# Attention then a gated feed-forward: four heads to a group, paired score matmuls, column-tiled values, and the two halves woven together

## Chip, cores, metric

One core of one Trainium2 chip. The metric is the device time of one execution in microseconds (us), the median of several runs.

## What is computed

Eight batches, 12 heads, 448 positions, head width 64, all inputs float32. The attention output, heads side by side (768 wide), feeds a gated feed-forward of inner width 1024. The result is float32, 8 x 448 x 768.

```python
q_n, k_n = rmsnorm(q, g_q), rmsnorm(k, g_k)        # over the head width
scores = (1 / sqrt(64)) * q_n @ k_n.T
attn = softmax(scores)
x = (attn @ v)                                      # heads side by side: 448 x 768
h = maximum(x @ w_in, 0)                            # 448 x 1024
u, v = h[..., :512], h[..., 512:]
v_n = (v - mean(v)) / sqrt(var(v) + 1e-6)
v_s = w_spatial @ v_n + b_spatial[:, None]          # mixes the 448 positions
out = (u * v_s) @ w_out
```

## The kernel before, in words

The kernel is written in a tile framework: the code gives the instructions, their tiles and an order of priority, and a scheduler fixes each engine's instruction queue ahead of the run. Each engine then works through its queue in order and waits on semaphores. Tiles come from pools with a fixed number of buffers. PE is TensorE, DVE VectorE, ACT ScalarE, POOL GpSimd, SP the queue that issues most DMAs.

It has two halves that follow each other. Constants and weights come first (L52 to L97): the weights are loaded as bfloat16 through POOL's DMA queue, and the spatial weights are transposed on TensorE.

*Attention* (L117 to L248) loops over batches and, inside, over heads. `prep_pair` (L118) loads q, k and v of two heads as bfloat16 with six POOL DMAs (L123, L126, L132), squares q and k on POOL (L143, L144), sums the squares on VectorE (L145, L148), takes Ln and Exp on ScalarE for the reciprocal root (L151, L153), scales q and k on VectorE (L162, L167), and transposes them on TensorE, two heads to 128 rows (L174, L179); VectorE copies them out of PSUM (L184, L185). A head's scores (L226) are four matmuls of 64 rows by 448 columns in two halves; the two matmuls of a half belong to the same head, so they use the same 64 rows of the array. ScalarE takes the exponential of each half (L232). No maximum is subtracted, since both operands are normalised. `emit_pv` (L191) multiplies by the values one head later: four matmuls whose stationary operand is 112 x 65, the 65th column being ones, so that row 64 of the result is the sum of the softmax (L195). The result leaves PSUM on ScalarE (L203) or VectorE (L206), and two SP DMAs carry it and the row of sums to DRAM (L207, L209).

*Between the halves* (L250 to L256) all sums are read back, inverted at once on VectorE, and written to DRAM.

*The gated half* (L266 to L360) loops over batches: x and the reciprocals, the latter broadcast to 64 rows each, are loaded from DRAM (L268 to L277) and multiplied (L279). `ps_uu` (L288) is u transposed, `ps_vv` (L306) is v; ScalarE applies Relu to both (L294, L312). VectorE takes the statistics (L315, L316), ScalarE Ln and Exp of the variance (L317, L319), VectorE normalises (L322). `ps_s` (L333) mixes the positions; the bias enters through a 113th row. VectorE multiplies by u (L339), `ps_oo` (L349) is the output projection, ScalarE copies it out (L355) and SP stores it (L357).

ScalarE's function tables are loaded by the compiler where a function is not in the active set; Ln and Exp alternate.

## Time and profile before

| | |
|---|---|
| three runs | 677.19, 679.34, 679.83 us (median 679.34) |
| span of the profiled execution | 677.2 us |
| PE busy | 548.9 us, 1936 matmuls |
| ACT busy | 388.2 us |
| POOL busy | 323.8 us |
| DVE busy | 277.4 us |
| DMA | 47.50 MB in 160417 packets |
| mean granted clock of PE | 0.979 |

The profiled execution's own time is its span from the first to the last instruction; no time outside it is listed. A line of the group list reads: source line, engine, operation, output <- inputs, shape of output <- input, count, then total busy us and mean ns of one, then the engine's idle time just before these instructions and what ended it. A line of a timeline reads: start in us, length in us, engine, line, operation, shape, count; several like instructions in a row are merged, and their length is from the first start to the last end. A matmul's end is modelled, so the distance between the starts of consecutive matmuls says more about the rate of the array than the length of one.

### The profile page before, as it was taken

How to read it: one execution, taken by the hardware profiler on the slowest of the kernel's cores; microseconds unless marked ns; L12 is line 12 of the kernel's file. 1: busy time of each engine (PE TensorE's matmuls, PEld its weight loads, DVE VectorE, ACT ScalarE, POOL GpSimd, SP SyncE). 2: the span in 40 equal slices, each digit the busy share in tenths (PEclk: the TensorE clock that was granted, in tenths of full speed). 3: DMA queues.
4: the chain of work that ended last, by engine and by line, in shares of the span. 5: the costliest groups of instructions: out<-in, count | busy, mean ns of one | idle time of the engine just before them, and what ended most of it. 6: DMA issues, size and time to landing. Idle time of an engine off the chain costs nothing.

```text
span 677.2 us, 6343 instructions
## 1 busy us (share of the span) xinstructions
PE 548.9 (81%) x1936; PEld 224.7 (33%) x1936; DVE 277.4 (41%) x519; ACT 388.2 (57%) x532; POOL 323.8 (48%) x452
## 2 busy tenths in 40 slices
PE   0167989798989989989979979992688898898875
PEld 0122332333333223233233223230344554464433
DVE  0167353643445355265255255232334234333331
ACT  0057676866876777676676686571244534544441
POOL 5799959595858867778678642002010011011000
PEclk9999999999999999999999999999988988999889
DMA  8978868675857776787577541002933532523022
GB/s 129 100 51 62 65 49 66 51 60 40 65 42 55 59 61 54 56 62 56 48 55 59 46 37 21 15 14 59 206 103 102 163 103 68 157 84 100 26 76 81
DMA packets 160417, 47.50 MB, mean 70 GB/s; under 512 B 136335, under 2 KB 156032, under 8 KB 160384
## 3 DMA queue, kind: packets, MB, share of 16 engines
q0 software_dynamic: 135520, 19.32, 41.2%
q1 hardware_dynamic: 24864, 27.79, 14.9%
q8 instruction: 15, 0.25, 0.1%
q14 instruction: 18, 0.15, 0.1%
HBM read 49.68 MB, written 16.69 MB: 98 GB/s over the span
## 4 chain that ended last, share of the span: by engine, by line
PE 61%; ACT 23%; DMA 6%; issue 4%; POOL 3%; DVE 2%; SPq 0%; DVEq 0%; ACTq 0%; POOLq 0%
PE ps_scores L226 20%; PE ps_o L195 18%; PE ps_s L333 6%; PE ps_oo L349 5%; PE ps_vv L306 5%; ACT L151 5%; ACT expT L232 5%; ACT L153 4%; PE ps_uu L288 4%; DMA w_sp_bf<-in_moe_w_spatial_dram 2%; DMA out_dram<-out_sb 2%; PE ps_t L179 2%; ACT lms_sb L151 2%; ACT out_sb L355 2%; PE ps_t L174 2%
## 5 line engine op out<-in xcount | busy, mean ns | idle before, releaser
L232 ACT ACTIVATE expT<-ps_scores 112x896 bf16<-112x896 f32 x192 | 174.0, 915 | 119.1 <-PE ps_scores L226 118.8
L226 PE MATMUL ps_scores<-qkT 64*112 64x448 bf16 x384 | 185.3, 592 | 27.1 <-ACT expT L232 14.5
L195 PE MATMUL ps_o<-expT,v_bf 112*65 112x448 bf16 x384 | 178.9, 579 | 2.9 <-ACT expT L232 2.8
L299 POOL MEMSET vn_sb<- 17x2048 bf16 x8 | 14.3, 1800 | 193.2 <-DVE xT_sb L279 112.3
L226 PEld LDWEIGHTS <-qkT 64*112 64x112 bf16 x384 | 53.3, 189 | 128.1 <-issue 101.0
L195 PEld LDWEIGHTS <-v_bf 112*65 112x65 bf16 x384 | 44.8, 155 | 103.8 <-issue 91.7
L355 ACT ACTIVATE out_sb<-ps_oo 112x768 f32<-112x768 f32 x32 | 26.0, 811 | 86.8 <-PE ps_oo L349 76.8
L132 POOL DMA_DIRECT2D v_bf<-in_v_dram x96 | 67.3, 706 | 12.7 <-DMA w_in_sb<-in_moe_w_in_dram 5.9
L206 DVE CAST xTu<-ps_o 65x448 bf16<-65x448 f32 x48 | 29.7, 619 | 103.4 <-PE ps_o L195 103.4
L123 POOL DMA_DIRECT2D q_raw<-in_q_dram x96 | 68.2, 710 | 5.0 <-DVE q_bf L162 2.6
L126 POOL DMA_DIRECT2D k_raw<-in_k_dram x96 | 69.2, 721 | 0.3
L333 PE MATMUL ps_s<-w_spT_sb,vn_sb 112*128 112x448 bf16 (+1 forms) x128 | 40.7, 463 | 23.7 <-DVE vn_sb L322 23.7
L288 PE MATMUL ps_uu<-xT_sb,w_in_sb 128*128 128x448 bf16 x192 | 44.6, 367 | 18.0 <-DVE xT_sb L279 18.0
L144 POOL TENSOR_TENSOR k_sq<-k_raw 112x512 bf16<-112x512 bf16 x48 | 50.9, 1060 | 16.4 <-DVE ms_sb L148 16.3
L143 POOL TENSOR_TENSOR q_sq<-q_raw 112x512 bf16<-112x512 bf16 x48 | 51.2, 1067 | 14.5 <-DVE ms_sb L145 14.1
L162 DVE SCALAR_TENSOR_TENSOR q_bf<-q_raw,rstd_sb 112x512 bf16<-112x512 bf16 x48 | 42.3, 882 | 26.7 <-ACT rstd_sb L153 25.0
L349 PE MATMUL ps_oo<-w_out_sb,gatedT_sb 128*112 128x384 bf16 x256 | 49.0, 326 | 4.9 <-ACT out_sb L355 4.7
L184 DVE COPY qkT<-ps_t 128x448 bf16<-128x448 bf16 x48 | 18.7, 389 | 83.4 <-PE ps_t L179 82.6
L315 DVE BATCH_NORM_STATS2 stats<-v_sb 112x6 f32<-112x512 bf16 x32 | 22.2, 693 | 66.6 <-ACT v_sb L312 66.6
L306 PE MATMUL ps_vv<-w_in_sb,xT_sb 128*112 128x512 bf16 x192 | 45.2, 379 | 0.4 <-ACT v_sb L312 0.4
L151 ACT ACT_TABLE_LOAD x34 | 43.6, 1283 | 1.3 <-PEq L375 0.7
L174 PE MATMUL ps_t<-identity,q_bf 112*128 112x112 bf16 x192 | 28.3, 295 | 17.8 <-DVE q_bf L162 17.7
(45 smaller groups left out, 511.8 us busy)
## 6 DMA issues: line engine op xcount, KB each, us to landing
out_dram<-out_sb SPq DMA_DIRECT2D x32, 336.0 KB, 2.7
v_bf<-in_v_dram POOLq DMA_DIRECT2D x96, 56.0 KB, 2.9
q_raw<-in_q_dram POOLq DMA_DIRECT2D x96, 56.0 KB, 2.7
k_raw<-in_k_dram POOLq DMA_DIRECT2D x96, 56.0 KB, 2.7
xT_dram<-xTu SPq DMA_DIRECT2D x96, 56.0 KB, 1.9
xT_sb<-xT_dram SPq DMA_DIRECT2D x8, 672.0 KB, 4.5
rec_bc<-rec_dram SPq DMA_DIRECT2D x16, 336.0 KB, 4.8
w_in_sb<-in_moe_w_in_dram POOLq DMA_DIRECT2D x1, 1536.0 KB, 11.5
```

What stands on the lines that cost most here:

```text
L123: pool_eng.dma_start(out=q_raw[:, :, hi, :], in_=q[b, hA + hi].rearrange("(c p) d -> p c d", p=P))
L126: pool_eng.dma_start(out=k_raw[:, :, hi, :], in_=k[b, hA + hi].rearrange("(c p) d -> p c d", p=P))
L132: pool_eng.dma_start(out=v_bf[:, hi, :, 0:D], in_=v[b, hA + hi].rearrange("(c p) d -> p c d", p=P))
L143: pool_eng.tensor_tensor(out=q_sq, in0=q_raw3, in1=q_raw3, op=ALU.mult)
L151: act.activation(out=lms_sb, in_=ms_sb, func=AF.Ln, bias=eps_col[0:P, :], scale=1.0 / D)
L195: pe.matmul(out=ps_o[:, 0:S], lhsT=v_bf[:, hi, jc, :], rhs=expT[:, jc, :], start=(jc == 0), stop=(jc == NCH - 1),)
L226: pe.matmul(out=ps_scores[:, jj, 0:S], lhsT=qkT_cur[p0:p0 + D, 1, jc * P:(jc + 1) * P], rhs=qkT_cur[p0:p0 + D, 0, :], start=True, stop=True,)
L232: act.activation(out=expT[:, 2 * half:2 * half + 2, :], in_=ps_scores[:, :, 0:S], func=AF.Exp, bias=0.0, scale=1.0,)
L288: pe.matmul(out=ps_uu, lhsT=w_in_sb[:, hc, ft * 128:(ft + 1) * 128], rhs=xT_sb[:, hc, :], start=(hc == 0), stop=(hc == NHD - 1),)
L306: pe.matmul(out=ps_vv, lhsT=xT_sb[:, hc, tcc * P:(tcc + 1) * P], rhs=w_in_sb[:, hc, DHALF:DF], start=(hc == 0), stop=(hc == NHD - 1),)
L333: pe.matmul(out=ps_s, lhsT=vn_sb[0:kp, sc, dt * 128:(dt + 1) * 128], rhs=w_spT_sb[0:kp, sc, :], start=(sc == 0), stop=(sc == NCH - 1),)
L349: pe.matmul(out=ps_oo[:, half, 0:DM // 2], lhsT=gatedT_sb[:, dc, tcc * P:(tcc + 1) * P], rhs=w_out_sb[:, dc, half * (DM // 2):(half + 1) * ...
```

## The change

It is a rewrite of the whole kernel function.

- Heads are handled in groups of four, three groups to a batch (24 in all); group g of a batch takes heads g, g+3, g+6 and g+9. q and k are loaded as float32 by SP, one DMA each for a group, three groups ahead; v by POOL, one DMA for a batch. Positions are split so that a partition holds four neighbouring ones, 1 KB in one piece.
- POOL squares q and k and also scales them (both on 1024 float elements of a partition at a time); VectorE sums the squares.
- The two score matmuls issued together now belong to the two heads of a pair, on rows 0 to 63 and 64 to 127 of the array, each into its own bank of PSUM; one exponential serves both.
- The sums come from separate matmuls with a stationary block of ones, 112 x 32, and the values from two half-width calls; each such call is 16 matmuls, four heads on four strips of 32 columns. The reciprocal is Exp(-Ln(sum)) on ScalarE, and VectorE multiplies by it as it takes the values out of PSUM. x stays on chip; the trip through DRAM and the stage between the halves are gone.
- ScalarE's table set is preloaded by name, one that has both Ln and Exp. Relu moves to VectorE.
- The gated part of a batch is cut into 21 units (v, normalisation, u, spatial, output), which are put into the instruction order between the steps of the next batch's attention: each of a group's eight steps adds 0.8 to an allowance, and units are taken while it is above zero, each subtracting its own figure. The first units are taken at the fifth step of the group after the batch's last. The last batch's units run alone at the end.
- PSUM is divided once: two score tiles of two banks, four one-bank tiles for all other uses.

Cut to its core:

```diff
--- before.py
+++ after.py
...
+    act.preload_act_table_set("natural_log_exp_and_others")
...
+    ps_sc = ctx.enter_context(tc.tile_pool(name="ps_sc", bufs=2, space=PSUM))
+    ps_w = ctx.enter_context(tc.tile_pool(name="ps_w", bufs=4, space=PSUM))
...
+    def load_qk(G):
+        b, g = divmod(G, NG)
+        qf = qk_pool.tile([P, 4, NC * D], FP, name="qf")
+        kf = qk_pool.tile([P, 4, NC * D], FP, name="kf")
+        sync.dma_start(out=qf, in_=q_g[b][g])
+        sync.dma_start(out=kf, in_=k_g[b][g])
+        raw[G] = (qf, kf)
...
-                for half in range(2):
-                    ps_scores = ps_sc.tile([P, 2, 512], FP, name="ps_scores")
-                    for jj in range(2):
-                        jc = 2 * half + jj
-                        pe.matmul(
-                            out=ps_scores[:, jj, 0:S],
-                            lhsT=qkT_cur[p0:p0 + D, 1, jc * P:(jc + 1) * P],
-                            rhs=qkT_cur[p0:p0 + D, 0, :],
-                            start=True, stop=True,
-                        )
-                    act.activation(
-                        out=expT[:, 2 * half:2 * half + 2, :],
-                        in_=ps_scores[:, :, 0:S],
-                        func=AF.Exp, bias=0.0, scale=1.0,
-                    )
...
+    def squares(G, i):
+        if i == 0:
+            sqs[G] = st_pool.tile([P, 2, 16], FP, name="ms")
+        t = sq_pool.tile([P, 4, NC * D], FP, name="sqt")
+        pool.tensor_tensor(out=t, in0=raw[G][i], in1=raw[G][i], op=ALU.mult)
+        dve.tensor_reduce(out=sqs[G][:, i, :],
+                          in_=t.rearrange("p l (c d) -> p (l c) d", d=D),
+                          axis=AX.X, op=ALU.add)
+    def rstd(G):
+        ln = st_pool.tile([P, 2, 16], FP, name="lnms")
+        rs = st_pool.tile([P, 2, 16], FP, name="rs")
+        act.activation(out=ln, in_=sqs[G], func=AF.Ln, bias=eps[0:P, :], scale=1.0 / D)
+        act.activation(out=rs, in_=ln, func=AF.Exp, bias=0.0, scale=-0.5)
+        rst[G] = rs
+    def scaled(G, i):
+        t = qn_pool.tile([P, NC, 4, D], BF, name=f"n{i}")
+        pool.tensor_tensor(
+            out=t.rearrange("p c l d -> p l c d"),
+            in0=raw[G][i].rearrange("p l (c d) -> p l c d", d=D),
+            in1=rst[G][:, i, :].rearrange("p (l c) -> p l c", c=NC).to_broadcast([P, 4, NC, D]),
+            op=ALU.mult)
+        nrm[G, i] = t
+    def transposes(G, pr):
+        ps = ps_w.tile([128, 8, 128], BF, name="ps")
+        for i in range(2):
+            for c in range(NC):
+                pe.matmul(out=ps[:, 4 * i + c, 0:P],
+                          lhsT=nrm[G, i][:, c, 2 * pr:2 * pr + 2, :],
+                          rhs=ident[0:P, 0:P], is_transpose=True,
+                          start=(i == 0 and c == 0), stop=(i == 1 and c == NC - 1))
+        t = qt_pool.tile([128, 2, NC, P], BF, name=f"qkt{pr}")
+        dve.tensor_copy(out=t[:, 0], in_=ps[:, 0:4, 0:P])
+        dve.tensor_scalar(out=t[:, 1], in0=ps[:, 4:8, 0:P], scalar1=g2_col, scalar2=None,
+                          op0=ALU.mult)
+        qkt[G, pr] = t
...
+    def scores(G, n):
+        pr, c = divmod(n, NC)
+        ps = ps_sc.tile([P, 2, 512], FP, name="pss")
+        t = qkt[G, pr]
+        for h in range(2):
+            pe.matmul(out=ps[:, h, 0:S],
+                      lhsT=t[64 * h:64 * h + 64, 1, c, :],
+                      rhs=t[64 * h:64 * h + 64, 0, :, :].rearrange("p c s -> p (c s)"),
+                      start=True, stop=True)
+        sct[G, n] = ps
+    def expo(G, n):
+        pr, c = divmod(n, NC)
+        if c == 0:
+            exps[G, pr] = e_pool.tile([P, NC, 2, S], BF, name="et")
+        act.activation(out=exps[G, pr][:, c, :, :], in_=sct[G, n][:, :, 0:S],
+                       func=AF.Exp, bias=0.0, scale=1.0)
...
+    def sums(G):
+        ps = ps_w.tile([128, 512], FP, name="ps")
+        for c in range(NC):
+            for l in range(4):
+                pe.matmul(out=ps[32 * l:32 * l + 32, 0:S], lhsT=ones,
+                          rhs=exps[G, l // 2][:, c, l % 2, :],
+                          start=(c == 0), stop=(c == NC - 1), tile_position=(0, 32 * l))
+        lr = r_pool.tile([128, S], FP, name="lr")
+        rc = r_pool.tile([128, S], FP, name="rc")
+        act.activation(out=lr, in_=ps[:, 0:S], func=AF.Ln, bias=0.0, scale=1.0)
+        act.activation(out=rc, in_=lr, func=AF.Exp, bias=0.0, scale=-1.0)
+        rec[G] = rc
+    def values(G, half):
+        b, g = divmod(G, NG)
+        if g == 0 and half == 0:
+            xts[b] = x_pool.tile([128, 6, S], BF, name="xt")
+        ps = ps_w.tile([128, 512], FP, name="ps")
+        for c in range(NC):
+            for l in range(4):
+                pe.matmul(out=ps[32 * l:32 * l + 32, 0:S],
+                          lhsT=vb[b][:, 3 * l + g, c, 32 * half:32 * half + 32],
+                          rhs=exps[G, l // 2][:, c, l % 2, :],
+                          start=(c == 0), stop=(c == NC - 1), tile_position=(0, 32 * l))
+        dve.tensor_tensor(out=xts[b][:, 2 * g + half, :], in0=ps[:, 0:S], in1=rec[G], op=ALU.mult)
...
+    def unit_v(b, c):
+        if c == 0:
+            vs[b] = m_pool.tile([P, NC, DH], BF, name="vs")
+            sts[b] = m_pool.tile([P, NC, 2], FP, name="mv")
+        ps = ps_w.tile([128, 512], FP, name="ps")
+        for j in range(6):
+            pe.matmul(out=ps[0:P, :], lhsT=xts[b][:, j, c * P:(c + 1) * P],
+                      rhs=w_in[:, j, DH:DF], start=(j == 0), stop=(j == 5))
+        dve.tensor_relu(out=vs[b][:, c, :], in_=ps[0:P, :])
+        s6 = st_pool.tile([P, 6], FP, name="s6")
+        dve.bn_stats(out=s6, in_=vs[b][:, c, :])
+        dve.bn_aggr(out=sts[b][:, c, :], in_=s6)
+    def unit_ln(b):
+        lv = st_pool.tile([P, NC], FP, name="lv")
+        rv = st_pool.tile([P, NC], FP, name="rv")
+        act.activation(out=lv, in_=sts[b][:, :, 1], func=AF.Ln, bias=eps[0:P, :], scale=1.0)
+        act.activation(out=rv, in_=lv, func=AF.Exp, bias=0.0, scale=-0.5)
+        for c in range(NC):
+            dve.tensor_scalar(out=vn_t[b % 2][0:P, c, :], in0=vs[b][:, c, :],
+                              scalar1=sts[b][:, c, 0:1], scalar2=rv[:, c:c + 1],
+                              op0=ALU.subtract, op1=ALU.mult)
...
+    def unit_o(b, c, half):
+        if half == 0:
+            osb[b, c] = o_pool.tile([P, DM], FP, name="osb")
+        ps = ps_w.tile([128, 512], FP, name="ps")
+        for f in range(4):
+            pe.matmul(out=ps[0:P, 0:384], lhsT=gts[b][:, f, c * P:(c + 1) * P],
+                      rhs=w_out[:, f, 384 * half:384 * half + 384],
+                      start=(f == 0), stop=(f == 3))
+        act.activation(out=osb[b, c][:, 384 * half:384 * half + 384], in_=ps[0:P, 0:384],
+                       func=AF.Copy, bias=0.0, scale=1.0)
+        if half == 1:
+            sync.dma_start(out=out[b].rearrange("(p c) m -> c p m", c=NC)[c], in_=osb[b, c])
...
+    NGT = B * NG
+    work = deque()
+    def moe_units(b):
+        for c in range(NC):
+            work.append((1.35, lambda c=c: unit_v(b, c)))
+        work.append((0.0, lambda: unit_ln(b)))
+        for f in range(4):
+            work.append((1.2, lambda f=f: unit_u(b, f)))
+        for f in range(4):
+            work.append((0.8, lambda f=f: unit_s(b, f)))
+        for c in range(NC):
+            for h in range(2):
+                work.append((0.66, lambda c=c, h=h: unit_o(b, c, h)))
+    def prep(G):
+        squares(G, 0)
+        squares(G, 1)
+        rstd(G)
+        scaled(G, 0)
+        scaled(G, 1)
+    prep(0)
+    load_weights()
+    prep(1)
+    transposes(0, 0)
+    scores(0, 0)
+    scores(0, 1)
+    transposes(0, 1)
+    debt = 0.0
+    for G in range(NGT + 1):
+        for n in range(8):
+            if G < NGT:
+                expo(G, n)
+                m, Gn = (n + 2) % 8, G + (n + 2) // 8
+                if Gn < NGT:
+                    scores(Gn, m)
+            if n == 0 and G + 3 < NGT:
+                load_qk(G + 3)
+            if n == 0 and G % NG == 0 and G // NG + 1 < B:
+                load_v(G // NG + 1)
+            if G > 0:
+                if n == 0:
+                    sums(G - 1)
+                elif n == 1:
+                    values(G - 1, 0)
+                elif n == 2:
+                    values(G - 1, 1)
+            if G + 1 < NGT:
+                if n == 3:
+                    transposes(G + 1, 0)
+                elif n == 5:
+                    transposes(G + 1, 1)
+            if G + 2 < NGT:
+                if n == 0:
+                    squares(G + 2, 0)
+                elif n == 1:
+                    squares(G + 2, 1)
+                elif n == 3:
+                    rstd(G + 2)
+                elif n == 4:
+                    scaled(G + 2, 0)
+                elif n == 6:
+                    scaled(G + 2, 1)
+            if G == 1 and n >= 4:
+                w_sp_unit(n - 4)
+            if G > 0 and G % NG == 0 and n == 4:
+                moe_units(G // NG - 1)
+            debt += 0.8
+            while work and debt > 0:
+                cost, fn = work.popleft()
+                debt -= cost
+                fn()
+            debt = min(debt, 0.8)
+    while work:
+        work.popleft()[1]()
```

The units that are left out, `unit_ln`, `unit_u` and `unit_s`, have the matmuls of the old gated half, in the same shapes; `unit_u` has Relu on VectorE.

More of the change, by code (lines that the diff above doesn't have):

```diff
@@ L2 @@
 import math
+from collections import deque
 from contextlib import ExitStack
@@ L6 @@
 import concourse.tile as tile
-from concourse import bass_utils, mybir
+from concourse import mybir
 from concourse.masks import make_identity
@@ L14 @@
 ALU = mybir.AluOpType
+AX = mybir.AxisListType
+PSUM = bass.MemoryType.PSUM
 @with_exitstack
```

365 lines of the change are left out of this document (90 added, 275 removed).

## The prediction

> **What bounds the kernel now.** I read the page first, then the group list with shapes apart, then one line's instructions, then short timelines of TensorE, and the stage windows last. The page:
>
> ```profile
> span 677.2 us, 6343 instructions
> PE 548.9 (81%) x1936; PEld 224.7 (33%) x1936; DVE 277.4 (41%) x519; ACT 388.2 (57%) x532; POOL 323.8 (48%) x452
> ...
> PE 61%; ACT 23%; DMA 6%; issue 4%; POOL 3%; DVE 2%; SPq 0%; DVEq 0%; ACTq 0%; POOLq 0%
> ```
>
> TensorE is the busiest engine and holds 61% of the chain that ended last, ScalarE 23%. A busy TensorE may still be a slow one, so the next views ask at what rate it runs: the score line's instructions, a stretch of the chain in order of time, and TensorE's timeline in attention.
>
> ```profile
> L226 PE MATMUL ps_scores<-qkT x384: 527/577/620, 39.3 to 458.4; 64*112 64x448 bf16 x192
> ```
> ```profile
> 429.98 1.49 PE ps_o L195 x4
> ```
> ```profile
> 431.40 0.99 PE L226 MATMUL ps_scores<-qkT 64*112 64x448 bf16 x2
> 432.32 0.95 PE L195 MATMUL ps_o<-expT,v_bf 112*65 112x448 bf16 x2
> 433.21 0.99 PE L226 MATMUL ps_scores<-qkT 64*112 64x448 bf16 x2
> ```
>
> Attention lasts from 39.3 to 458.4, so 4.37 us a head for 96 heads. Four matmuls of 448 columns take 1.49 us, 0.373 each. Two of scores and two of values come round in 433.21 - 431.40 = 1.81 us; less 4 x 0.373 that leaves 0.32 us, 0.16 for each change between the 64-row and the 112-row shape. The same engine in the gated half:
>
> ```profile
> 602.46 1.46 PE L349 MATMUL ps_oo<-w_out_sb,gatedT_sb 128*112 128x384 bf16 x8
> 603.75 4.05 PE L306 MATMUL ps_vv<-w_in_sb,xT_sb 128*112 128x512 bf16 x18
> 607.64 2.81 PE L288 MATMUL ps_uu<-xT_sb,w_in_sb 128*128 128x448 bf16 x14
> 613.22 1.06 PE L333 MATMUL ps_s<-w_spT_sb,vn_sb 112*128 112x448 bf16 x4 [2.77 <-DVE vn_sb L322]
> ```
>
> Here 18 matmuls of 512 columns take 607.64 - 603.75 = 3.89 us, 0.216 each; in proportion 448 columns cost 0.189, half of attention's 0.373; eight of 384 take 1.29, 0.161 each. So attention runs at half the array rate. No score matmul there is shorter than 527 ns, so it never changes. The window view:
>
> ```profile
> 430.00:460.00 30.00, 28.61 (x77) 8.74 (x76) 7.23 (x14) 20.90 (x27) 0.00 (x0) 1.00 0.06 14
> ```
>
> The clock column says 1.00 for that stretch, which the spacing contradicts; I go by spacing. PE is busy 28.61 of 30 us and still slow. By the Trainium skill ("TensorE: Matmul & The Clock Gate", Part 1) some 3.4 us of sustained activity release the full clock; the trace disagrees for 420 us. By that rule the woven part would be fast, as forecast below, and the groups without gated work would drop from 12 us to nearer ScalarE's 8.2, some 13 us in all. My own reading is that the filled part of the array counts: a score matmul holds 64 of 128 rows, a value matmul 65 of 128 columns, the gated ones nearly all.
>
> **The change, per batch of three groups (12 heads).** All terms are at the full rate first.
>
> TensorE. Scores: 48 matmuls, issued as pairs on rows 0-63 and 64-127; if a pair runs together, 24 x 0.189 = 4.5 us (9.1 if not; no row shows two at once). Shape changes: scores interrupt other work 24 times, two changes each, and nine column-tiled calls add about six: 54 x 0.16 = 8.6 us, taken as the slow clock showed it, with 0 as the lower end. The Trainium skill ("TensorEngine Tiling (Array Packing)", Key Properties) says that a change of tiling mode drains the engine: a rule against this change, and the 0.16 agrees. Sums and values: three calls a group of 16 matmuls on four 32-column strips, 144 in all; if four run together, 36 x 0.189 = 6.8 us, else 27.2. The Trainium skill ("TensorE: Matmul & The Clock Gate", Part 3) gives 2.38x for three strips; by that share of the ideal the 6.8 would be an estimated 8.6, and no run here shows it. I take 6.8. Transposes: 48, priced from
>
> ```profile
> 206.12 0.56 PE L174 MATMUL ps_t<-identity,q_bf 112*128 112x112 bf16 x4
> 206.47 0.58 PE L179 MATMUL ps_t<-identity,k_bf 112*128 112x112 bf16 x4
> ```
>
> as 0.35/4 = 0.088 slow, 0.044 if halved; I take 0.075, 3.6 us. Gated part: 24 x 0.216 + 24 x 0.189 + 16 x 0.189 + 32 x 0.161 = 17.9 us. Sum 41.4 us, 13.8 a group; without shape changes 32.8, 10.9 a group. The rows for the other engines:
>
> ```profile
> L232 ACT ACTIVATE expT<-ps_scores 112x896 bf16<-112x896 f32 x192 | 174.0, 915 | 119.1 <-PE ps_scores L226 118.8
> L151 ACT ACT_TABLE_LOAD x34 | 43.6, 1283 | 1.3 <-PEq L375 0.7
> L153 ACT ACT_TABLE_LOAD x24 | 30.8, 1283 | 0.4
> L355 ACT ACTIVATE out_sb<-ps_oo 112x768 f32<-112x768 f32 x32 | 26.0, 811 | 86.8 <-PE ps_oo L349 76.8 <-DMA out_dram<-out_sb 6.1 <-PE ps_vv L306 3.9
> L203 ACT ACTIVATE xTu<-ps_o 65x448 bf16<-65x448 f32 x48 | 25.9, 539 | 1.0 <-PE ps_o L195 1.0
> ...
> L151 ACT ACTIVATE lms_sb<-ms_sb,eps_col 112x16 f32<-112x16 f32 x48 | 13.2, 303 | 33.7 <-DVE ms_sb L148 33.3
> L232 ACT ACT_TABLE_LOAD x10 | 12.8, 1283 | 0.6 <-PE ps_scores L226 0.4
> L317 ACT ACT_TABLE_LOAD x8 | 10.3, 1283 | 0.1
> L319 ACT ACT_TABLE_LOAD x8 | 10.3, 1283 | 0.1
> L153 ACT ACTIVATE rstd_sb<-lms_sb 112x16 f32<-112x16 f32 x48 | 8.7, 209 | 0.3
> ```
> ```profile
> 205.48 1.73 ACT L232 ACTIVATE expT<-ps_scores 112x896 bf16<-112x896 f32 x2
> ```
>
> ScalarE. Back to back the 915 ns exponential costs 1.73 - 0.915 = 0.82. Per batch 24 x 0.82 = 19.6; three reciprocals as Ln and Exp at 0.54 each, 3.2; four small Ln-Exp pairs at 0.303 + 0.209, 2.0; eight half-width output copies, between 0.41 (half of 811) and 0.54, say 0.48, 3.8. Sum 28.6 us, 9.5 a group. The 84 table loads (108 us) go, if the one preloaded set serves Ln and Exp; Relu moves to VectorE.
>
> ```profile
> L145 DVE TENSOR_REDUCE ms_sb<-q_sq 112x8 f32<-112x512 bf16 x48 | 32.5, 678 | 22.3 <-POOL q_sq L143 11.6 <-ACT lms_sb L151 10.7
> ...
> L315 DVE BATCH_NORM_STATS2 stats<-v_sb 112x6 f32<-112x512 bf16 x32 | 22.2, 693 | 66.6 <-ACT v_sb L312 66.6
> L185 DVE TENSOR_SCALAR qkT<-ps_t,g2g_col 128x448 bf16<-128x448 bf16 x48 | 21.2, 442 | 0.0
> L339 DVE SCALAR_TENSOR_TENSOR gatedT_sb<-ps_s,uT_sb 128x448 bf16<-128x448 f32 x32 | 20.0, 624 | 14.8 <-PE ps_s L333 14.3
> L184 DVE COPY qkT<-ps_t 128x448 bf16<-128x448 bf16 x48 | 18.7, 389 | 83.4 <-PE ps_t L179 82.6
> ...
> L322 DVE TENSOR_SCALAR vn_sb<-v_sb,mv_sb,rstd_ln 112x512 bf16<-112x512 bf16 x32 | 11.1, 410 | 25.9 <-ACT rstd_ln L319 25.9
> L316 DVE BATCH_NORM_AGGREGATE mv_sb<-stats 112x2 f32<-112x6 f32 x32 | 5.8, 182 | 1.1
> ```
> ```profile
> L143 POOL TENSOR_TENSOR q_sq<-q_raw 112x512 bf16<-112x512 bf16 x48 | 51.2, 1067 | 14.5 <-DVE ms_sb L145 14.1
> ```
>
> VectorE. Six sums of squares over 1024 elements at up to 2 x 0.678, 8.1; six pairs of 0.389 + 0.442, 5.0; 18 reads of PSUM at 0.624 (the two value halves of each group, four Relu of u, four products, four Relu of v), 11.2; four of 0.693 + 0.182 + 0.410, 5.1. Sum 29.4 us, 9.8 a group. POOL: squares and scaling are 12 products of 1024 float elements at 2 x 1.067 = 2.13, so 25.6 us, 8.5 a group; if float elements cost double the bf16 ones, 51 us, 17 a group. By the Trainium skill ("GPSIMD Engine Reference", Performance versus the Vector engine), 4497 ns for 2048 float elements, the estimate would be 2.25 us each and 27 us a batch; no run here shows float. I take 25.6. The loads of q and k leave POOL's queue for SP's, where only the output stores stand with them; they are issued three groups ahead, so SP waiting for a free buffer holds stores, not TensorE, unless stores fall four tiles behind.
>
> So per woven group PE needs 13.8, DVE 9.8, ACT 9.5, POOL 8.5: PE sets the pace if its clock is full. It is kept full by nearly filled tiles; even a 2.77 us pause left the four matmuls after 613.22 at 1.06 us together, less than the 1.49 of the slow rate. I take 13.8, since a cheaper shape change and the waits of engines for each other pull opposite ways. The gated part begins at the middle of group 3, so 3.5 groups run without it. At the slow rate they cost PE 8 x 0.373 + 18 x 0.16 + 12 x 0.373 + 16 x 0.088 = 11.7 us each, against ScalarE's 8 x 0.82 + 0.5 + 1.1 = 8.2; I take 12.
>
> Ends. The transfer nearest in size:
>
> ```profile
> xT_sb<-xT_dram SPq DMA_DIRECT2D x8, 672.0 KB, 4.5
> ```
>
> The first q and k, 448 KB each, are 896 KB together: in proportion 6 us. Then four POOL products (8.5), a reduction (1.4), Ln and Exp (0.5), transposes and copies (1.5), and weight-DMA issues between (3): first exponential at about 21 us, where the first scores now start at 39.3. Behind the last group stand sums and values (4), then a whole gated batch alone: v 5.2, u 4.5, spatial 3.0, output 5.2, two dependent hand-overs of about 1 and the last copy and store, 3.3: 27 us together. x, rowsums and reciprocals no longer pass through DRAM, so the idle stretch between the halves disappears.
>
> Sum: 21 + 3.5 x 12 + 20.5 x 13.8 + 27 = 373 us against the profiled span of 677.2. The three runs are 677.19, 679.34 and 679.83, up to 2.6 above that span; adding 2 for the median gives 375.
>
> **Rivals.** *Engines in lockstep, or POOL at double price.* Two score buffers, four shared PSUM buffers and in-order queues make one engine wait for another: at 17 us a group (POOL's upper end) 21 + 42 + 349 + 27 = 439. For it: ACT, DVE and PE are within a third of each other, so little slack covers a late release. Against: the next group's preparation is issued a group or two ahead.
>
> *The clock stays low in the woven part.* PE needs 24 x 0.373 + 8.6 + 36 x 0.373 + 48 x 0.088 + 35.6 = 70.8 us a batch, 23.6 a group; with ten more at the end, 21 + 42 + 484 + 37 = 584. For: 420 us of attention never sped up. Against: gated matmuls sped up within their first stage, and now half of PE's work is these.
>
> *Column strips run one after another at full clock.* Then 108 more slots x 0.189 = 20.4 a batch, 20.6 a group: with 6.8 for each early group, 21 + 66 + 422 + 30 = 539.
>
> *Strips one after another, and their quarter-filled array holds the clock low: slower than before.* 70.8 + 108 x 0.373 = 111.1 a batch, 37 a group; early groups 25: 21 + 88 + 759 + 40 = 908. It decides the sign above (677 - 21 - 42 - 37)/20.5 = 28 us a woven group, that is when fewer than about two strips run together at the slow clock. For: values alone already left half the array idle and slow. Against: strips write separate partitions and have separate weights.
>
> *The table set does not stay.* 14 loads a batch x 1.283 = 18 us on ACT, 15.5 a group before waits; with 3 us of waits 18.5, and 16 for early groups: 21 + 56 + 379 + 29 = 485.
>
> **How the numbers follow.** Forecast 0.60, lockstep 0.19, low clock 0.07, strips in turn at full clock 0.06, strips in turn at low clock 0.04, table loads 0.04. The forecast's own range is 325 (no shape-change cost, 11.4 a group) to 410 (15.6). Reaching to lockstep and table loads makes 325 to 485; low clock, both strip cases and the outer edge of the forecast are left out, about 0.2. A difference of 0.5% is about what a measurement of this kernel can tell. Faster than that: all but the low-clock strips and a little of unknown mishap, 0.94; within it 0.01; slower 0.05.
>
> **What would show it.** Right: 448-column matmuls 0.19 us apart in the woven stretch; both matmuls of a score pair, and four strips, starting almost together; one or two table loads; POOL products near 2.1 us; first exponential near 21 us; PE on most of the chain; a batch every 41 us. Wrong: spacing of 0.37 after the third group, strips 0.19 apart, POOL products of 4 us, or score matmuls whose wait is put down to ACT in most steps.

## The result and the profile after

The changed kernel takes 410.64 us (median of four runs, 409.48 to 411.57) against 678.91 for the kernel before (four runs, 677.19 to 679.83): a ratio of 0.605, 95% interval 0.603 to 0.606. The forecast was 375 in a range of 325 to 485. A run more than 1.5% above the fastest of its kernel is left out of medians and ratios, which concerns one run of all that are told here. From the page of the changed kernel, its span, the busy times and the chain that ended last:

```profile
span 409.8 us, 6684 instructions
PE 332.8 (81%) x2704; PEld 155.4 (38%) x2704; DVE 214.4 (52%) x394; ACT 231.5 (57%) x369; POOL 192.0 (47%) x116
...
PE 36%; POOL 23%; DMA 16%; issue 12%; DVE 10%; ACT 3%; POOLq 0%; DVEq 0%
```

Every engine lost work, TensorE most (548.9 to 332.8). TensorE holds only 36% of the chain, where before it held 61%; POOL and DMA hold 39%. The forecast had PE on most of it, so the kernel is faster, but PE's pace is not what bounds it throughout. TensorE's timeline in a late stretch (start, us, tile, count) answers the question of rate:

```profile
345.96 0.40 PE L186 MATMUL pss<-qkt 64*112 64x448 bf16 x2
346.29 0.94 PE L206 MATMUL ps<-et,ones 112*32 112x448 bf16 x16
347.16 0.86 PE L283 MATMUL ps<-w_out,gt 128*112 128x384 bf16 x4
347.95 0.40 PE L186 MATMUL pss<-qkt 64*112 64x448 bf16 x2
348.28 0.94 PE L222 MATMUL ps<-et,vt 112*32 112x448 bf16 x16
```

Both matmuls of a pair are over in 0.40 us (unpaired, an experiment below shows, they take 0.58). The 16 matmuls on four strips take 0.94, of which 0.37 is the last one's own length; the rest is three steps of 0.19. So four strips share one slot of 448 columns at the full rate. The Trainium skill ("TensorE: Matmul & The Clock Gate", Part 3) has 2.38x for three strips, by whose share of the ideal the forecast estimated 8.6 us a batch. The trace shows four strips in one slot, which is 4x and the 6.8 of the forecast, and the measurement decides.

Shape changes are read from the same lines: from the scores at 345.96 to the strips is 0.33, against the 0.19 of a slot, so 0.14; from the strips at 346.29 to the output matmuls it is 0.87, against four slots or 0.76, so 0.11. The trace has 411 changes; over those at the full rate with no wait before the next matmul the means are 0.095 into scores, 0.133 from scores, 0.095 out of strips. By the Trainium skill ("TensorEngine Tiling (Array Packing)", Key Properties) a change of mode drains the engine; the trace agrees in that a change costs time, about 0.11 us each, less than the 0.16 taken.

The windows, for a middle and a late stretch (columns: window, length, busy PE, PEld, DVE, ACT, POOL, clock, DMA share, GB/s):

```profile
160.00:220.00 60.00, 52.99 (x448) 25.15 (x448) 29.78 (x57) 39.42 (x66) 29.21 (x16) 0.97 0.43 111
...
310.00:370.00 60.00, 60.00 (x530) 28.16 (x528) 34.05 (x73) 42.97 (x61) 11.28 (x6) 1.00 0.11 33
```

In the middle PE stands idle for 7 of 60 us and does 448 matmuls; late it does 530 with no idle time. From the starts of every eighth exponential a group takes 15.4 us in the middle (groups 5 to 17, 14.3 to 16.8) and 12.6 to 13.1 in the last five. What differs is POOL and DMA: the last load of q and k has landed by then (its squares run at 294.9). So 12.6 is about what PE needs, and the middle pays some 2.8 us a group for something that comes with the loads. The waits name it (waiter, releaser: total us, count, longest):

```profile
POOL n L155 <- PE ps L166: 91.6, 17, 9.7
DVE ms L142 <- POOL sqt L141: 82.3, 27, 7.5
ACT lnms L149 <- DVE ms L142: 68.7, 17, 26.3
...
POOL sqt L141 <- DMA qf<-in_q_dram: 32.2, 14, 2.6
```

The squares wait for a load, VectorE's reduction waits for the squares, and the reduction holds ScalarE's Ln (26.3 of its 68.7 is the start). One instance, from the timelines of POOL, VectorE, ScalarE and PE (in brackets the idle time before, and its releaser):

```profile
218.00 1.89 POOL L141 TENSOR_TENSOR sqt<-qf 112x1024 f32<-112x1024 f32 x1 [2.63 <-DMA qf<-in_q_dram]
221.37 1.89 POOL L141 TENSOR_TENSOR sqt<-kf 112x1024 f32<-112x1024 f32 x1 [1.48 <-DMA kf<-in_k_dram]
```
```profile
219.93 1.22 DVE L142 TENSOR_REDUCE ms<-sqt 112x16 f32<-112x1024 f32 x1 [7.48 <-POOL sqt L141]
221.06 0.61 DVE L226 TENSOR_TENSOR xt<-ps,rc 128x448 bf16<-128x448 f32 x1
223.30 1.22 DVE L142 TENSOR_REDUCE ms<-sqt 112x16 f32<-112x1024 f32 x1 [1.62 <-POOL sqt L141]
```
```profile
224.55 0.32 ACT L149 ACTIVATE lnms<-ms,eps 112x32 f32<-112x32 f32 x1 [4.06 <-DVE ms L142]
224.78 1.70 ACT L196 ACTIVATE et<-pss 112x896 bf16<-112x896 f32 x2
```
```profile
225.10 2.51 PE L237 MATMUL ps<-w_in,xt 128*112 128x512 bf16 x7 [2.13 <-DVE xt L226]
227.54 0.62 PE L186 MATMUL pss<-qkt 64*112 64x448 bf16 x2
```

SP issued that q load at about 213.5, when POOL had scaled group 14 and so freed its raw buffer. The load is group 18's, and POOL's next instruction is already the squares of group 18. It waits for the transfer; VectorE stands 7.48 us at the reduction, and the two products of x (L226) stand behind it and behind the next reduction, though their matmuls had ended by 218.37 and 220.35; ScalarE stands 4.06 at the Ln, with two ready exponentials behind; PE then waits 2.13 for x. None of the three waits concerns work that is due: attention is in group 12. In the program's text the squares of G+2 stand in group G's slots; in the trace they run four groups before their own scaling, as many as there are raw buffers, so the scheduler that orders the program's steps has moved them up as far as buffers allow (six groups with six buffers, below).

Such a wait has an aftermath that the last line above shows: a pair takes 0.62 us again, and the granted clock is 0.50 from 225.9 to 229.3. From the first woven work on the trace has five stretches like this (at 82.5, 96.2, 178.1, 225.9 and 253.2), 20.4 us in all. At half the rate they cost PE at most about 10 us, an estimate.

The start, from the timelines of POOL and VectorE:

```profile
5.50 1.89 POOL L141 TENSOR_TENSOR sqt<-qf 112x1024 f32<-112x1024 f32 x1 [2.00 <-DMA qf<-in_q_dram]
7.35 1.89 POOL L141 TENSOR_TENSOR sqt<-kf 112x1024 f32<-112x1024 f32 x1
```
```profile
13.40 0.16 DVE L98 SCALAR_TENSOR_TENSOR g_col<-gq_col,gk_col 128x1 f32<-128x1 f32 x1 [8.09 <-DMA gk_col<-in_g_k_dram]
25.32 0.55 DVE L120 CAST w_spT<-bst 17x448 bf16<-17x448 f32 x1 [11.76 <-DMA bst<-in_moe_b_spatial_dram]
25.90 2.35 DVE L142 TENSOR_REDUCE ms<-sqt 112x16 f32<-112x1024 f32 x2
```

The squares were done at 9.2, and the reduction begins at 25.90: it stands in VectorE's order behind two small steps whose loads (g and the spatial bias) land late. The first exponential starts at 34.8 instead of 21.

**The theory from this, and its rivals.** Theory: the run-ahead preparation sits at the head of in-order queues and costs the middle its 2.8 us a group. Rivals: too few buffers (raw q and k, or scaled ones) make POOL and the loads late; or the 15.4 is the price of the transfers themselves; or the packing on PE does less than the slots say. For the start: the small loads behind the big ones, or v and the weights sharing the DMA engines with the first q and k.

### The profile page after: what moved, and what is told of

The parts are those of the page before. It is cut to its first block, busy times and chain, and to the rows that moved or that the text cites. A ratio compares the mean times of both kernels' runs of the same rounds, so it can differ in the third digit from the quotient of the medians.

```text
span 409.8 us, 6684 instructions
## 1 busy us (share of the span) xinstructions
PE 332.8 (81%) x2704; PEld 155.4 (38%) x2704; DVE 214.4 (52%) x394; ACT 231.5 (57%) x369; POOL 192.0 (47%) x116
## 3 DMA queue, kind: packets, MB, share of 16 engines
q0 software_dynamic: 12368, 8.27, 14.3%
## 4 chain that ended last, share of the span: by engine, by line
PE 36%; POOL 23%; DMA 16%; issue 12%; DVE 10%; ACT 3%; POOLq 0%; DVEq 0%
POOL n L155 11%; POOL sqt L141 10%; DMA qf<-in_q_dram 9%; PE ps L283 7%; DMA kf<-in_k_dram 7%; PE pss L186 6%; PE ps L237 6%; PE ps L259 5%; DVE ms L142 4%; PE ps L166 3%; PE ps L222 3%; PE ps L271 3%; DVE xt L226 3%; PE ps L206 2%; ACT et L196 2%
## 5 line engine op out<-in xcount | busy, mean ns | idle before, releaser
L196 ACT ACTIVATE et<-pss 112x896 bf16<-112x896 f32 x192 | 171.6, 914 | 46.7 <-PE pss L186 46.4
L142 DVE TENSOR_REDUCE ms<-sqt 112x16 f32<-112x1024 f32 x48 | 58.2, 1217 | 82.7 <-POOL sqt L141 82.3
L155 POOL TENSOR_TENSOR n<-qf,rs 112x1024 bf16<-112x1024 f32 x24 | 45.6, 1900 | 112.9 <-PE ps L166 91.6
L186 PE MATMUL pss<-qkt 64*112 64x448 bf16 x384 | 79.7, 417 | 5.1 <-ACT et L196 3.1
L141 POOL TENSOR_TENSOR sqt<-qf 112x1024 f32<-112x1024 f32 x24 | 45.4, 1890 | 32.3 <-DMA qf<-in_q_dram 32.2
L237 PE MATMUL ps<-w_in,xt 128*112 128x512 bf16 x192 | 50.3, 403 | 10.7 <-DVE xt L226 10.7
L283 PE MATMUL ps<-w_out,gt 128*112 128x384 bf16 x256 | 52.2, 334 | 4.8 <-DVE gt L274 4.8
L186 PEld LDWEIGHTS <-qkt 64*112 64x112 bf16 x384 | 25.7, 129 | 65.5 <-issue 58.5
L141 POOL TENSOR_TENSOR sqt<-kf 112x1024 f32<-112x1024 f32 x24 | 45.3, 1889 | 8.0 <-DMA kf<-in_k_dram 7.8
L222 PE MATMUL ps<-et,vt 112*32 112x448 bf16 x768 | 48.7, 366 | 0.0
L149 ACT ACTIVATE lnms<-ms,eps 112x32 f32<-112x32 f32 x24 | 7.8, 324 | 68.7 <-DVE ms L142 68.7
L155 POOL TENSOR_TENSOR n<-kf,rs 112x1024 bf16<-112x1024 f32 x24 | 45.6, 1899 | 0.0
L226 DVE TENSOR_TENSOR xt<-ps,rc 128x448 bf16<-128x448 f32 x48 | 29.6, 616 | 26.3 <-PE ps L222 25.0
```

Source lines behind the costliest of these rows:

```text
L141: pool.tensor_tensor(out=t, in0=raw[G][i], in1=raw[G][i], op=ALU.mult)
L142: dve.tensor_reduce(out=sqs[G][:, i, :], in_=t.rearrange("p l (c d) -> p (l c) d", d=D), axis=AX.X, op=ALU.add)
L155: pool.tensor_tensor(out=t.rearrange("p c l d -> p l c d"), in0=raw[G][i].rearrange("p l (c d) -> p l c d", d=D), in1=rst[G][:, i, :].rear ...
L186: pe.matmul(out=ps[:, h, 0:S], lhsT=t[64 * h:64 * h + 64, 1, c, :], rhs=t[64 * h:64 * h + 64, 0, :, :].rearrange("p c s -> p (c s)"), star ...
L196: act.activation(out=exps[G, pr][:, c, :, :], in_=sct[G, n][:, :, 0:S], func=AF.Exp, bias=0.0, scale=1.0)
L222: pe.matmul(out=ps[32 * l:32 * l + 32, 0:S], lhsT=vb[b][:, 3 * l + g, c, 32 * half:32 * half + 32], rhs=exps[G, l // 2][:, c, l % 2, :], s ...
```

## Experiments

All ratios are to the kernel before, with 95% intervals.

**Small loads first.** The DMAs of g_q, g_k and the bias move ahead of the first q and k on SP's queue.

```diff
+    sync.dma_start(out=gq_col, ...)
+    sync.dma_start(out=gk_col, ...)
+    sync.dma_start(out=bst[96:113, :], in_=moe_b_spatial.partition_broadcast(17))
...
     load_qk(0)
...
```

> The three small loads (g_q, g_k, the spatial bias) are issued ahead of the first q and k on SP's queue. In the changed kernel VectorE's queue stands from 5.3 to 13.4 us for g_k and again to 25.3 for the bias, while the first squares are done at 9.2. Theory 1 (the start is lost to these two waits and is kept to the end): first exponential at about 19 us instead of 34.8, total 410.6 - 15 = about 395. Theory 2 (POOL, busy 40.9 of the 43 us after the first exponential, or the loads of groups 1 to 3 take over): first exponential earlier, but less than 8 us gained in all, 403 or more.

Measured 403.26 us (402.0 to 403.84), 0.593 (0.591 to 0.594): 7.4 less. The first exponential starts at 26.4 instead of 34.8. The gain has a limit, seen in POOL's timeline of this kernel:

```profile
12.46 1.89 POOL L142 TENSOR_TENSOR sqt<-qf 112x1024 f32<-112x1024 f32 x1 [8.96 <-DMA qf<-in_q_dram]
```

The first q is now squared at 12.46, where it was 5.50: the block on VectorE is gone, and the load has become late instead.

**Squares of a resident tile.** From group 3 on POOL squares a tile that was loaded once, so no squares wait for a load. The sums of squares, and so the scaling, are then wrong for later groups.

```diff
+        if G == 0:
+            still.append(const.tile([P, 4, NC * D], FP, name="still"))
+            sync.dma_start(out=still[0], in_=q_g[0][0])
...
-        pool.tensor_tensor(out=t, in0=raw[G][i], in1=raw[G][i], op=ALU.mult)
+        x = raw[G][i] if G < 3 else still[0]
+        pool.tensor_tensor(out=t, in0=x, in1=x, op=ALU.mult)
```

> From group 3 on POOL squares a tile that is loaded once (q of group 0) instead of the group's own q and k; loads, products, reductions, Ln and Exp all stay, so the norms are not those of the group. Theory A (reductions and Ln-Exp of a group far ahead stand early in the in-order queues of VectorE and ScalarE and wait there for squares that wait for loads): the groups of the middle go from 15.4 us to 13.3 or less, as the last six run at 12.6, total about 385. Theory B (it is the work of the preparation, 2.4 us of reductions and 0.55 of Ln-Exp a group, not a wait): 408 to 412.

Measured 392.91 us, 0.578 (0.576 to 0.579): 17.7 less. Groups 7 on take 12.6 to 13.6; group 4 takes 20.0 (18.2 in the changed kernel) and group 6 20.7. In group 6 POOL runs seven squares without a break (13.00 us from 123.80), now free of loads; VectorE's reductions follow at POOL's pace, and the products of x stand behind them. So run-ahead work can still hold due work. VectorE's wait for squares falls from 82.3 to

```profile
DVE ms L146 <- POOL sqt L145: 25.4, 17, 3.7
```

So the middle's excess is the wait on loads, and neither PE nor the transfers themselves: those still run, all of them.

**More buffers.** One kernel has four scaled pairs instead of two, another six raw pairs instead of four.

```diff
-    qn_pool = ctx.enter_context(tc.tile_pool(name="qn", bufs=2))
+    qn_pool = ctx.enter_context(tc.tile_pool(name="qn", bufs=4))
```
```diff
-    qk_pool = ctx.enter_context(tc.tile_pool(name="qk", bufs=4))
+    qk_pool = ctx.enter_context(tc.tile_pool(name="qk", bufs=6))
```

> Four buffers instead of two for the scaled q and k, so that POOL's scaling waits less for the transposes that free a buffer (91.6 us of POOL's idle time). Theory A with the wait at this place: q and k tiles come free earlier, loads go out earlier, squares come in time: 390 to 400. Theory A with the wait at the loads, or theory B: POOL only waits elsewhere, 406 to 412.

> Six buffers instead of four for the loaded q and k, so that a load need not wait for the scaling of four groups before. Theory A with the wait at the loads (POOL waits 40 us for them in all): 390 to 400. If the scheduler only places the squares still further ahead, or by theory B: 406 to 412.

Four scaled pairs: 416.53 us, 0.611 (0.609 to 0.614), 5.9 more than the changed kernel; group 4 alone takes 25.2 instead of 18.2, and why is open. Six raw pairs: 408.36, 0.600 (0.599 to 0.602), hardly less. Groups 5 to 15 take 15.8 and 15.4 us on average, where the changed kernel takes 15.5, and the wait stays where it was; first the one, then the other:

```profile
DVE ms L142 <- POOL sqt L141: 78.2, 26, 7.6
```
```profile
DVE ms L142 <- POOL sqt L141: 72.0, 25, 7.8
```

With six raw pairs the squares run six groups ahead instead of four, again right behind a load that was just issued. More room does not give slack here, since the order takes it up at once. Too few buffers for raw or for scaled tiles, each by itself, are refuted as the cause.

**A short lead.** The small statistics (the mean squares, their Ln, the reciprocal root) get one buffer instead of three, so that one group's reduction can't be placed ahead of the Ln of the group before it. Nothing else changes.

```diff
+    sx_pool = ctx.enter_context(tc.tile_pool(name="sx", bufs=1))
-            sqs[G] = st_pool.tile([P, 2, 16], FP, name="ms")
+            sqs[G] = sx_pool.tile([P, 2, 16], FP, name="ms")
...
-        ln = st_pool.tile([P, 2, 16], FP, name="lnms")
-        rs = st_pool.tile([P, 2, 16], FP, name="rs")
+        ln = sx_pool.tile([P, 2, 16], FP, name="lnms")
+        rs = sx_pool.tile([P, 2, 16], FP, name="rs")
```

> One buffer instead of three for the sums of squares, their Ln and their reciprocal root, so that VectorE's reduction and ScalarE's Ln-Exp of a group can stand at most one group or two ahead of POOL's scaling, not four. Theory A (VectorE and ScalarE lose time because their early entries wait for squares that wait for a load just issued): the entries now stand behind squares that are done; middle groups 15.4 -> about 13.5, total 380 to 390. Theory B (the work of the preparation itself) or a wait that only moves again, as with more buffers: 405 to 415.

Measured 380.72 us (379.42 to 381.86), 0.560 (0.559 to 0.562): 29.9 less, by taking two buffers of each away. The chain, three rows of the waits, and a middle window of this kernel:

```profile
PE 55%; POOL 23%; issue 12%; DVE 5%; ACT 3%; DMA 1%; POOLq 0%; DVEq 0%
```
```profile
DVE ms L143 <- ACT lnms L150: 35.6, 13, 3.9
...
POOL sqt L142 <- DMA qf<-in_q_dram: 27.6, 11, 3.6
...
DVE ms L143 <- POOL sqt L142: 9.0, 8, 3.7
```
```profile
160.00:220.00 60.00, 58.30 (x505) 27.80 (x505) 42.18 (x80) 41.61 (x67) 35.65 (x21) 1.00 0.54 122
```

DMA's share of the chain falls from 16% to 1%, the wait for squares from 82.3 to 9.0, and PE does 505 matmuls in the window instead of 448. VectorE now waits 35.6 us for ScalarE's Ln, a wait that delays little. A middle group takes 13.2 on average. The squares still run four groups ahead, and POOL still waits 27.6 us for q. But the reductions now stand some 12 us behind (the squares of group 18 run at 198.29, their reduction at 209.92), so they find the squares done. The falls of the clock are gone too: it is 1.00 from 67 to 376, so a part of the gain is theirs. This is the theory's case, and it is shown: the same transfers, fewer buffers, only the order differs.

With six raw pairs besides:

> The short lead and six instead of four buffers for the loaded q and k: loads go out two groups ahead of the squares, squares four ahead of the scaling, reductions one or two. Theory A: POOL's 38 us of waiting for loads vanish as well and the middle groups come to 13, total 378 to 388, below the short lead alone by up to 5. Theory B: 405 to 415.

379.99 us, 0.560 (0.557 to 0.563): the same within the interval. POOL's wait for q falls to 1.6 us, so what it waits with four buffers costs nothing.

**Scores not paired.** Both score matmuls of a step belong to one head and stand on the same 64 rows, so they can't run together; the exponential writes its result where the pair's would have gone, and the work is the same.

```diff
-        pr, c = divmod(n, NC)
+        pr, r = divmod(n, NC)
+        h, half = divmod(r, 2)
...
-        for h in range(2):
+        for j in range(2):
+            c = 2 * half + j
...
```

> The two score matmuls issued together belong to one head again and use the same 64 rows, as in the kernel before; all else as in the changed kernel. If two row halves really run together (the forecast's 24 slots a batch), a group now needs 8 x 0.189 = 1.5 us more of TensorE: the last six groups go from 12.6 to 14.1, and the total rises by 9 us if the middle groups' waits absorb it, by up to 24 x 1.5 = 36 if they do not: 420 to 447. If they never ran together: 408 to 413.

Measured 429.59 us (426.97 to 430.6; a fourth run, 433.75, is the one left out), 0.631 (0.628 to 0.634): 19.0 more than the changed kernel. A late pair of scores in PE's timeline of this kernel:

```profile
367.42 0.58 PE L188 MATMUL pss<-qkt 64*112 64x448 bf16 x2
```

It takes 0.58 where the paired one took 0.40. In the last five groups, where PE sets the pace, a group takes 14.1 on average instead of 12.7, as 8 x 0.18 = 1.4 has it. In the middle the difference is small, as the wait on loads covers it there.

The rest comes from the clock. The starts of matmuls tell more of it than the clock column, which has 1.00 from 46 to 60 in the changed kernel, where PE is busy 12.96 of 14 us and a pair takes 0.62 (the mean of 0.979 given for the kernel before has the same fault, as its attention ran at half rate). So the paired kernel begins at half rate too. From 61.83 on its PE has nothing but pairs and strips, and at 65.52 a pair takes 0.40; its PE timeline:

```profile
64.10 0.62 PE L186 MATMUL pss<-qkt 64*112 64x448 bf16 x2
...
65.52 0.40 PE L186 MATMUL pss<-qkt 64*112 64x448 bf16 x2
```

Unpaired, PE has nothing but scores and strips from 65.24 to 75.30, and the rate stays halved; its timeline, and the window before its gated work begins (91.7):

```profile
74.37 0.99 PE L188 MATMUL pss<-qkt 64*112 64x448 bf16 x2
```
```profile
60.00:88.00 28.00, 28.00 (x147) 9.32 (x146) 15.41 (x22) 16.20 (x24) 23.59 (x13) 0.50 0.28 77
```

Unpaired, PE is busy 28.00 of 28 us and granted half the clock until about 96, when gated work has begun (a pair takes 0.58 from 97.1 on). Groups 2 and 3 take 15.9 and 17.5 instead of 9.9 and 14.5. By the Trainium skill ("TensorE: Matmul & The Clock Gate", Part 1) some 3.4 us of sustained activity release the full clock; the paired stretch of 3.7 us agrees, but neither the unpaired window nor the old kernel's 420 us bear that out if activity means busy time. It fits activity counted over the filled part of the array, as the forecast read it. What exactly is counted is not shown.

**No table preloaded.** The line that loads the table set of Ln and Exp is left out.

> The table set is not preloaded by name; all else as in the changed kernel. Table loads come back at about 112 (14 a batch) x 1.283 = 144 us of ScalarE, 6 us a group on top of 9.5. Where ScalarE has slack (15.4 - 9.5 = 5.9 a group) they are half hidden: 430 to 500 by the forecast's rival, 410 to 415 if ScalarE's slack hides all.

470.2 us (two runs), 0.691 (0.688 to 0.694): 59.6 more. 108 table loads come back; of ScalarE's groups two:

```profile
L210 ACT ACT_TABLE_LOAD x24 | 30.8, 1283 | 0.4
L148 ACT ACT_TABLE_LOAD x22 | 28.2, 1283 | 1.1 <-PEq L382 0.7
```

The rival priced at 485 was this case, 15 us too dear. The clock has a share in the price: this kernel pairs its scores too, but PE is busy only 22.02 us of the 28 from 60 to 88, and the granted clock is 0.50 there. In the changed kernel there is one load:

```profile
L45 ACT ACT_TABLE_LOAD x1 | 1.3, 1283 | 0.7 <-PEq L383 0.7
```

**The start, with v and w_in held back.** To the short lead come the small loads first; v and w_in are held back until the first mean squares exist, by a small write from them into the tiles that the DMAs fill.

```diff
...
+    dve.tensor_copy(out=vb[0][:, 0, 0, 0:1], in_=sqs[0][:, 0, 0:1])
+    dve.tensor_copy(out=w_in[0:P, 0, 0:1], in_=sqs[0][:, 0, 0:1])
     rstd(0)
     scaled(0, 0)
     scaled(0, 1)
+    load_v(0)
```

> The short lead (380.7 us, first exponential at 36.1) with another start: g_q, g_k and the bias first on SP's queue, then q and k of group 0, and v of batch 0 and the big input weights held back until the first sums of squares are there. Putting the small loads first had the first q land at 12.4 us instead of 5.4, with v and weights in flight beside it. Theory 1 (two things hold the start: VectorE's queue behind small loads, and first q and k sharing the DMA engines with v and weights): first exponential at about 19, total about 364. Theory 2 (only the small loads): first exponential near 26, total about 371. If groups 1 to 3 wait for the loads put off: 375 or more.

370.32 us (369.91 to 371.73), 0.545 (0.544 to 0.547): the best of all, 40.3 below the changed kernel. The first exponential starts at 26.0 (36.1 with the short lead alone). But the first q came no earlier; POOL's timeline of this kernel:

```profile
14.45 1.89 POOL L142 TENSOR_TENSOR sqt<-qf 112x1024 f32<-112x1024 f32 x1 [12.04 <-DMA qf<-in_q_dram]
```

With v and w_in out of the way q is still squared at 14.45, so sharing with these two is refuted as the cause of the late q. It was not alone, though: the scheduler moved w_sp's load (392 KB) up to 1.29, and that landed 6.2 us later. The small loads ahead of q remain the likeliest cause, which is not shown: VectorE uses the bias at 8.98 in the small-loads kernel and at 12.52 here, and q is squared 3.5 and 1.9 us after it. Which of them, g's or the bias's, holds the queue was not tried, nor q first with the two VectorE steps placed later.

**Values right behind the sums.** On top of the short lead the three calls with strips are put together, which takes PE's shape changes from 411 to 351.

```diff
                 if n == 0:
                     sums(G - 1)
-                elif n == 1:
                     values(G - 1, 0)
-                elif n == 2:
                     values(G - 1, 1)
```

> The short lead (380.7 us), with the two value calls of a group issued right behind its sums instead of one and two steps later. TensorE's queue then changes between 64-row, 32-column and full shape 351 times instead of 411. If a change costs the 0.13 us that the starts in the changed kernel show, and TensorE sets the pace: 60 x 0.13 = 8 us less, 373. If changes are free, or ScalarE now waits for scores behind a longer run of strips: 379 to 388.

382.62 us, 0.563 (0.561 to 0.564), no gain over 380.72. Sixty changes less are worth 60 x 0.11 = 6.6 us on PE, but a middle group (7 to 17) takes 13.5 instead of 13.2: PE's wait for exponentials rises from 6.9 to 11.2, and VectorE's wait for the reciprocal before a product of x from 7.2 to 25.3. Scores that come often seem to be what keeps ScalarE fed; this was not tried by itself. All edits together:

> Short lead, new start and strips together. If the gains are of separate stretches they add: 380.7 - 17 - 8 = about 356. If one of them is covered by the others: 362 to 372.

371.73 us, 0.547 (0.546 to 0.549): no better than without this one.

**Gated work not woven.** On top of the short lead all gated work comes after all attention; eight x tiles and fewer buffers elsewhere make room for it.

```diff
-            if G > 0 and G % NG == 0 and n == 4:
-                moe_units(G // NG - 1)
...
+    for b in range(B):
+        moe_units(b)
```

> The short lead (380.7 us), with all gated units issued after the last batch's attention (x of all batches stays on chip; to make room v has two buffers, the reciprocals one, the outputs two). Groups of attention alone at about 10, as groups 1 and 2 of the changed kernel: 36 + 24 x 10 = 276, then 8 x 18 = 144 of gated work and an end of 3: about 423 if the packed attention alone brings the full clock; 36 + 24 x 11.7 + 147 = 464 if it stays at the slow one, as the attention of the kernel before did. 385 or less if weaving is worth nothing.

396.69 us (two runs), 0.583 (0.582 to 0.585): only 16 more than the woven one; I expected 423, and this miss is the most telling. Its two stages:

```profile
80.00:240.00 160.00, 159.55 (x1619) 63.24 (x1620) 89.99 (x156) 157.96 (x242) 139.48 (x78) 1.00 0.54 114
240.00:394.00 154.00, 147.42 (x803) 89.17 (x801) 92.03 (x194) 34.98 (x84) 0.00 (x0) 1.00 0.24 72
```

Attention alone takes 7.9 us a group with ScalarE busy 157.96 of 160, so ScalarE sets the pace there; I had taken 10. (PE shows busy too, but its ends are modelled and its scores wait in step with the exponentials.) The gated part takes 154 us for eight batches, 19.2 each, little above the 17.9 of its slots. Packed attention keeps the full clock by itself (a pair takes 0.40 from 72.63 on), so weaving isn't needed for that. Weaving fills ScalarE's time with PE's work: start, attention and the rest take 36 + 205 + 153 here, against 36 + 313 + 29 with weaving.

## Why the prediction was right, and where its sizes were off

The sign was right, and 410.64 lies in the range, 36 above the number. Part of that is the width of the range: the forecast's own ended at 410, and it was reached to 485 for two rivals. What TensorE would do was right in the main; what would wait was not. The terms, on the profiled execution (the early groups end at the fifth exponential of group 3, the woven ones with the last exponential):

| term | forecast | measured |
|---|---|---|
| first exponential | 21 | 34.8 |
| 3.5 early groups | 42 | 41.7 |
| 20.5 woven groups | 283 (13.8 each) | 304.6 (14.9 each) |
| end | 27 | 28.7 |
| sum | 373 | 409.8 |

**Right.** Pairs run together: undoing that costs 1.4 us a group where PE is the bound. Strips run four at a time. The preloaded set serves Ln and Exp: without it 60 us return. The clock is full in the woven part but for the five stretches after waits; the forecast, which saw a pause of 2.77 us leave it full, had none of these. Of the signs named in advance, the first exponential near 21, PE on most of the chain and a batch every 41 us (about 45) did not come. POOL's float products take the lower price, 1.89 us, not double:

```profile
L141 POOL TENSOR_TENSOR sqt<-qf 112x1024 f32<-112x1024 f32 x24 | 45.4, 1890 | 32.3 <-DMA qf<-in_q_dram 32.2
```

**The early groups, partly by luck.** They were priced at 12 each, at the slow rate. That rate lasted only to 65.5, and groups 1 and 2 took 10.2 and 9.9; group 0 took 16.9, as PE waited for POOL's scaled tiles, and made the sum come out.

**The start, 13.8 short.** The step that failed is "then four POOL products (8.5), a reduction (1.4)": the reduction does not follow the products, it stands behind two steps that wait for small loads. Moving these gave 7.4 us of it. The forecast's 6 us for the transfer held in the changed kernel (squares from 5.50), so what remains in the start kernel is the late q.

**The woven groups, two errors of opposite sign.** PE's need was too high. Shape changes are 17.1 x 0.11 = 1.9 a group, not 2.9; a transpose takes 0.049, not 0.075. With them 8 x 0.189 + 1.9 + 12 x 0.189 + 16 x 0.049 + 17.9/3 = 12.4, close to the 12.6 to 13.1 of the last groups. Against that stood the waits, 15.4 less 12.6. The forecast said that a cheaper shape change and "the waits of engines for each other pull opposite ways", and set them equal; the one was worth 1.4 and the other 2.8. The sentence that failed is the one against the lockstep rival: "the next group's preparation is issued a group or two ahead". It is issued four ahead, and that is no slack but the cause: each step waits for a load that has just been sent, at the head of a queue that holds due work. The rival was half right: engines do wait for each other in order, by another mechanism and at 15.4 instead of 17. The short lead, which changes only this order, gave 29.9 us, and with the start mended 370.32: the forecast's number was near what the change can do without these two blocks, partly by errors that cancel.

## What to carry to other kernels

Look at what stands at the head of each in-order queue, not at how busy the engine is: work prepared far ahead blocks due work as soon as it waits for a transfer, and more buffers only move it further ahead. Bound the lead of a side chain by the buffers of its smallest tiles, and keep steps that wait for small loads off the queue of an engine that the first tile needs. Before weaving two stages together, price each by its own bound, since the gain is only what the one leaves idle under the other.

## What the runs showed of the hardware that was not expected

With three small loads ahead of it on SP's queue a 448 KB load was used at 12.46 us instead of 5.50, and at 14.45 with v and w_in held back and w_sp's load in flight; why is open. Half-filled attention was granted 0.50 of the clock at 28.00 busy of 28 us; filled attention came to the full rate at 65.52 us and kept 1.00 through 160 us without gated work. After waits of PE in the woven part the granted clock was 0.50 for 3.4 to 6.8 us, five times. A change of the matmul's shape costs 0.095 to 0.133 us, and 16 matmuls on four strips end within 0.94 us.
